# Chunked attention before a token mixer: batch 0's third tile reordered, and its first weights decoded later

## The chip, the cores and the metric

The kernel runs on one core of a Trainium2 chip. The metric is the device time of one execution in microseconds; it is compared between the kernel before and the kernel after. The engines are named as the profile names them: PE (matrix multiplications, with PEld for the loading of its weights), DVE (vector), ACT (activation), POOL and SP (which issues most of the DMA).

## The reference

Four batches of 8 heads, 768 positions, head size 64. Attention works in chunks of 32 positions, and what it gives goes through a token mixer of low rank and a two-layer network.

```
for each chunk of 32 positions c:
    k_full = [mem_k, k[c-16 : c+40]];  v_full = [mem_v, v[c-16 : c+40]]
    a = softmax(q_c @ k_full.T / 8)
    x[c] = a @ v_full
u   = x + (x.T @ U @ V).T          # U: 768x32, V: 32x768
out = u + relu(u @ w_ch1) @ w_ch2  # 512 -> 2048 -> 512
```

U, V, w_ch1 and w_ch2 reach the chip as 64-bit floats and are decoded on the chip, from two 32-bit words each, into a value that is held as a high part and a low part.

## The kernel before

The work is laid out in four batches. Batch 0's attention has the chip to itself at the start. From then on the network of a batch (`w1_step` and `w2_step`, lines 1235 to 1296) runs on PE while the attention of the next batch is woven into it. Products that need more than the low precision are done in three passes (high with high, high with low, low with high), so x's transposed form `u` and the weights both exist as a pair (`uh`, `ul`; `w1h`, `w1l`).

A batch has 6 blocks of 128 positions, taken in three tiles T = 0, 1, 2 of two blocks each. For a tile, `s_turn` makes the scores (line 551, 128 small matmuls on tiles of the PE array), `s_weights` the exponentials (L573 to L577), `s_sums` the row sums and their reciprocals (L582 to L587), `t_part` turns the exponentials in two calls (L605 on PE, L608 on ACT), and `av_part` makes the products with v (L624, again small matmuls, as many as for the scores) and scales them into two blocks of x on DVE (L635, four instructions). `collect(t)` adds block t of x times U into one bank (L647). V is decoded by `v_words` on ACT and DVE (L199, L206, L214, L219, L226) and spread over three groups of rows by `spread_v` (L251 on PE, L256 on ACT, L257 on DVE).

When all six blocks are collected, lines 921 and 922 split the sums into `g3`. The first half of u for the network (blocks 0 to 2) is then made in two steps: `turn_x` has turned x into four banks (L967), and `join_uT` adds V times g3 to them (L976) and splits each bank into `uh` (L980, ACT) and `ul` (L981, DVE). The second half (blocks 3 to 5) goes the same way by `turn_x1` (L991) and `join_uT1` (L1008, L1012, L1013); three of its four banks are done in the attention, the fourth in `joins`, inside the first `w1_step`.

The order of instructions on PE, ACT, DVE, POOL and SP is written out by hand here: an engine executes them in the order in which the program emits them. A waiting instruction holds back everything that comes after it on its engine. Three devices in this order matter:

- `keep_clock(n)` asks for n matmuls on zeros ahead of the next bank that is taken (L130). `GAP` and `CHAIN` hold the numbers.
- `bank()` gives out PSUM banks; while `wide[0]` is a number it goes round `cyc`, a list of seven entries over three pools, and with `None` it takes the three banks of `ps_a` alone.
- `stream()` decodes the network's weights, and `advance(n)` takes n steps of it. A word (one matrix of one f, or later both) goes through `begin` (ACT, L199), `shift` (DVE, L206), `power` (L214), `mantissa` (L219), `join` (L226), `upper` (ACT, L337: the high part) and `lower` (DVE, L341: the low part). Steps end where the code says `yield`. In the kernel before, `advance(5)` takes the first word through `join` and `upper` and begins the second; the two steps of `advance(2)` shift the second and make the first one's low part. `both_blocks` starts the network when `done[0]` says that both words of f = 0 are through.

The front's last part in the kernel before, in the order in which PE has it: scores of tile 2, `t_part(0)`, `av_part(0)`, `t_part(1)`, six matmuls on zeros, `av_part(1)`, `t_part(2)`, `collect` 0 to 3, `spread_v`, `turn_x`, two matmuls on zeros, `av_part(2)`, `collect` 4 and 5, two matmuls on zeros, `turn_x1` three times, then the joins.

Of the kernel before, what the change touches and what calls it, by code (L numbers as in the profile page):

```python
# [24 lines left out]
HEAD = {ET.Activation, ET.Pool}  # L25
FIRST = 3000
START = 12
GAP = [2, 2, 6, 2]
LOADS = 'mv t1 t2 uv v0 v1 v2 w0 w1 w2'
CHAIN = [2, 4]  # L30
WLO = 4
# [22 lines left out]
def chunk_attn_then_mixer_kernel(  # L54
# [56 lines left out]
    wide = [0]  # L111
# [15 lines left out]
    def att_ps():  # L127
        ps = bank()
        for _ in range(warm[0]):
            nc.tensor.matmul(out=ps, lhsT=busy[:, 0:P], rhs=busy, start=True, stop=True)  # L130
        warm[0] = 0
        return ps

    def keep_clock(n):

        warm[0] += n
# [110 lines left out]
    def spread_v(val):  # L247
        for g in range(VG):
            ps = att_ps()
            rows = slice(32 * g, 32 * g + 32)  # L250
            nc.tensor.matmul(  # L251
                out=ps[0:96, 0:VQ], lhsT=rep[rows].rearrange("p a b -> p (a b)"),
                rhs=val[rows, 0:VQ], start=True, stop=True,
            )
            c = slice(VQ * g, VQ * g + VQ)
            nc.scalar.copy(out=v3[:, c], in_=ps[0:96, 0:VQ])  # L256
            nc.vector.tensor_tensor(  # L257
                out=v3[32:64, c], in0=ps[32:64, 0:VQ], in1=v3[32:64, c].bitcast(F32), op=ALU.subtract,
            )
# [80 lines left out]
    def lower(f, which, val, hi, lo):  # L340
        nc.vector.tensor_tensor(out=lo, in0=val, in1=hi.bitcast(F32), op=ALU.subtract)  # L341
        if which == 0:
            unsaved.append((f, w1ls[f]))
        done[0] = 2 * f + which + 1

    done = [0]

    def stream():

        work = [[(f, n)] for f in range(NSOLO) for n in range(2)] + [[(f, 0), (f, 1)] for f in range(NSOLO, NF)]  # L350

        def ready(n):
            return n < len(work) and work[n][0][0] in staged and not (front[0] and len(work[n]) > 1)

        def begun(n):
            words = Words([raw for f, which in work[n] for raw in staged[f][which]], nc.vector, turn=n)
            words.begin()
            return words

        while not ready(0):  # L360
            yield
        ahead, before = begun(0), []
        yield
        for n, parts in enumerate(work):
            while ahead is None and not ready(n):
                yield
            if n + 1 == len(work):
                for part in before:
                    lower(*part)
                before = []  # L370
                yield
            words, ahead = ahead or begun(n), None
            words.shift()
            if before:
                yield
                for part in before:
                    lower(*part)
            if len(parts) > 1 and n + 2 < len(work) and ready(n + 1):
                ahead = begun(n + 1)
            yield  # L380
            words.power()
            yield
            words.mantissa()
            yield
            if ahead is None and n + 2 < len(work) and ready(n + 1):
                ahead = begun(n + 1)
            val = words.join()
            before = [(f, which, val[:, 512 * m:512 * m + 512]) for m, (f, which) in enumerate(parts)]
            before = [part + upper(*part) for part in before]
            yield  # L390
        for part in before:
            lower(*part)
        yield
# [3 lines left out]
    def advance(n):  # L397
        for _ in range(n):
            next(weights, None)
# [7 lines left out]
    def attention(b, xs):  # L407
# [129 lines left out]
        def s_turn(T):  # L537
            *_, last = s_halves(T)
            return last
# [39 lines left out]
        def s_sums(T):  # L579
            rs = rss[T] = sm.tile([P, 2, 2, 2, 2], F32, name="rs", bufs=3)  # L580
            for s in range(2):
                nc.vector.tensor_reduce(  # L582
                    out=rs[:, :, :, :, s].rearrange("n t g k -> n t k g"),
                    in_=pts[T, s].rearrange("n (t k g w) -> n t k g w", t=2, k=2, g=2), axis=AX.X, op=ALU.add,
                )
            nc.vector.tensor_scalar_add(out=rs, in0=rs, scalar1=1e-9)
            nc.vector.reciprocal(out=rs, in_=rs)  # L587
# [22 lines left out]
        def av_part(T):  # L610
            for _ in av_halves(T):
                pass
# [32 lines left out]
        def collect(t):  # L645
            if b == 0:
                nc.tensor.matmul(  # L647
                    out=gp[0][0:96], lhsT=u3[:, t].rearrange("p g r -> p (g r)"), rhs=xs[(b, t)],
                    start=(t == 0), stop=(t + 1 == NT),
                )  # L650
                return
            j = t % 4
            nc.tensor.matmul(  # L653
                out=gp[0][R * j:R * j + R, :], lhsT=u_sb[:, t, :], rhs=xs[(b, t)],
                start=(t < 4), stop=(t + 4 >= NT),
            )

        if b == 0:
# [59 lines left out]
            yield  # L718
            keep_clock(GAP[0])
            sc = s_turn(0)  # L720
# [7 lines left out]
            yield  # L728
            keep_clock(GAP[1])
            sc = s_turn(1)  # L730
# [14 lines left out]
            s_weights(2, *sc)  # L745
            v_words.begin()
            s_sums(1)
            av_part(0)
            yield
            for s in two:  # L750
                t_part(1, s)
            s_sums(2)
            keep_clock(GAP[2])
            av_part(1)
            for s in two:
                t_part(2, s)
            for t in two:
                collect(t)
            v_words.shift()
            v_words.low()  # L760
            val = v_words.join()
            yield
            for t in two:
                collect(2 + t)
            spread_v(val)
            early = turn_x(range(NCK))
            wide[0] = None
            keep_clock(GAP[3])
            av_part(2)
            yield  # L770
            advance(5)
            for t in range(4, NT):
                collect(t)
            keep_clock(CHAIN[0])
            turned.extend(turn_x1(c) for c in range(3))
            advance(2)
            yield
        else:
            mv = sm.tile([P, 4 * D], F32, name="mv")
# [139 lines left out]
        for c in range(0, CH, width):  # L919
# [3 lines left out]
                out=g3[64:96, cs], in0=gr[64:96, cs], in1=g3[64:96, cs].bitcast(F32), op=ALU.subtract,  # L923
            )
        if b == 0:
            join_uT(early, g3)
            for c in range(3):
                join_uT1(turned[c], c, g3)
            rest.extend((c, g3) for c in range(3, NCK))
            ranks.append(g3)  # L930
        yield "joined"
# [28 lines left out]
    def turn_x(cs):  # L960

        banks = []
        for c in cs:
            ps = ps_h.tile([P, 512], F32, name="ps_h") if c < 2 else ps_o.tile([P, 512], F32, name=f"acc{c - 2}")
            banks.append(ps)
            for tt in range(TB):
                nc.tensor.matmul(  # L967
                    out=ps[:, tt * P:(tt + 1) * P], lhsT=xs[(0, tt)][:, c * P:(c + 1) * P],
                    rhs=ident, start=(tt == 0), stop=False, skip_group_check=True,
                )  # L970
        return banks

    def join_uT(banks, g3):
        uht, ult = u_pair(0, 0)
        for c in range(NCK):
            nc.tensor.matmul(  # L976
                out=banks[c][:, 0:TOK], lhsT=g3[:, c * P:(c + 1) * P], rhs=v3[:, 0:TOK],
                start=False, stop=True, skip_group_check=True,
            )
            nc.scalar.copy(out=uht[:, c, :], in_=banks[c][:, 0:TOK])  # L980
            nc.vector.tensor_tensor(  # L981
                out=ult[:, c, :], in0=banks[c][:, 0:TOK], in1=uht[:, c, :].bitcast(F32), op=ALU.subtract,
            )

    turned, rest, ranks = [], [], []

    def turn_x1(c):

        ps = att_ps()
        for tt in range(TB):  # L990
            nc.tensor.matmul(  # L991
                out=ps[:, tt * P:(tt + 1) * P], lhsT=xs[(0, TB + tt)][:, c * P:(c + 1) * P],
                rhs=ident, start=(tt == 0), stop=False, skip_group_check=True,
            )
        return ps
# [8 lines left out]
    def join_uT1(ps, c, g3):  # L1004
        if (0, 1) not in uT:
            u_pair(0, 1)
        uh, ul = (a[c] for a in uT[(0, 1)])
        nc.tensor.matmul(  # L1008
            out=ps[:, 0:TOK], lhsT=g3[:, c * P:(c + 1) * P], rhs=v3[:, TOK:2 * TOK],
            start=False, stop=True, skip_group_check=True,  # L1010
        )
        nc.scalar.copy(out=uh, in_=ps[:, 0:TOK])  # L1012
        nc.vector.tensor_tensor(out=ul, in0=ps[:, 0:TOK], in1=uh.bitcast(F32), op=ALU.subtract)  # L1013
# [379 lines left out]
    head = ExitStack()  # L1393
    head.enter_context(tc.manual_schedule(engines=HEAD))
    first = attention(0, xs)
    base = tc.tile_snap_priority() - FIRST
    while True:
# [79 lines left out]
```

## Time and profile before

| what | value |
|---|---|
| median of 3 runs | 668.75 us (668.54, 668.75, 1119.33) |
| the profiled execution | 667.39 us |
| its span | 665.5 us |
| mean granted clock of PE | 0.991 |
| instructions profiled | 15136 |

The profiled execution is not one of the three runs. Its span lies between the first and the last profiled instruction; 1.9 us lie around it. Times in the trace are microseconds from the start of the span. A row of the timeline gives start, duration, engine, line, operation, output and inputs and how many were merged; in brackets stands how long the engine had been idle before and who ended that. The chain of waits follows the end of the program back through what released each step; "issue" there is time in which an engine waited for nothing that the profile shows. A row of the stretches gives, for each engine, busy time and count of instructions, and then PE's granted clock, the share of the DMA engines' time and what they moved.

### The profile page before, as it was taken

How to read it: one execution, taken by the hardware profiler on the slowest of the kernel's cores; microseconds unless marked ns; L12 is line 12 of the kernel's file. 1: busy time of each engine (PE TensorE's matmuls, PEld its weight loads, DVE VectorE, ACT ScalarE, POOL GpSimd, SP SyncE). 2: the span in 40 equal slices, each digit the busy share in tenths (PEclk: the TensorE clock that was granted, in tenths of full speed). 3: DMA queues.
4: the chain of work that ended last, by engine and by line, in shares of the span. 5: the costliest groups of instructions: out<-in, count | busy, mean ns of one | idle time of the engine just before them, and what ended most of it. 6: DMA issues, size and time to landing. Idle time of an engine off the chain costs nothing.

```text
span 665.5 us, 15136 instructions
## 1 busy us (share of the span) xinstructions
PE 641.1 (96%) x6192; PEld 559.4 (84%) x6192; DVE 343.1 (52%) x672; ACT 234.8 (35%) x574; POOL 72.6 (11%) x98
## 2 busy tenths in 40 slices
PE   8788999999979999999999989999999999999997
PEld 5557999998867898988878888999978899999886
DVE  6848788898552553435524733444536732222322
ACT  5526344447422244242322615332324512121221
POOL 5100000043000333051432000000000000000000
PEclk9899999999988999999999999999999999999999
DMA  8895366453850598456744378675523055555301
GB/s 235 154 330 197 126 203 204 129 160 113 161 133 18 173 290 249 109 171 218 235 159 158 128 230 248 188 198 138 158 79 111 1 158 167 157 157 160 120 1 47
DMA packets 121116, 105.98 MB, mean 159 GB/s; under 512 B 51192, under 2 KB 90616, under 8 KB 121048
## 3 DMA queue, kind: packets, MB, share of 16 engines
q1 hardware_dynamic: 120424, 104.87, 53.6%
q8 instruction: 49, 0.80, 0.5%
q10 hardware_dynamic: 624, 0.15, 0.1%
q14 instruction: 19, 0.16, 0.1%
HBM read 79.30 MB, written 25.17 MB: 157 GB/s over the span
## 4 chain that ended last, share of the span: by engine, by line
PE 88%; DVE 5%; DMA 2%; issue 2%; ACT 2%; SPq 0%; ACTq 0%; DVEq 0%
PE acc L1286 23%; PE ps_h L1235 19%; PE ps_h L1163 17%; PE acc L1296 11%; PE ps_a L624 2%; PE ps_a L492 2%; PE ps_a L551 2%; PE ps_a L1286 2%; PE ps_a L605 1%; DMA w1l<-w1s 1%; PE acc L1280 1%; PE ps_a L1296 1%; PE ps_a L653 1%; PE ps_a L1092 1%; PE ps_a L938 1%
## 5 line engine op out<-in xcount | busy, mean ns | idle before, releaser
L1286 PE MATMUL acc<-w,hh 128*128 128x512 f32 x606 | 158.6, 397 | 0.0
L1286 PEld LDWEIGHTS acc<-w,hh 128*128 128x128 f32 x606 | 110.6, 188 | 21.5 <-issue 1.3
L1296 PE MATMUL acc<-w,hl 128*128 128x512 f32 x303 | 87.4, 397 | 0.0
L1235 PE MATMUL ps_h<-uh,w1h 128*128 128x384 f32 x252 | 85.7, 342 | 0.6 <-ACT uh L1012 0.6
L1235 PE MATMUL ps_h<-ul,w1h 128*128 128x384 f32 x252 | 84.4, 337 | 0.4 <-DVE ul L1013 0.4
L1244 DVE SCALAR_TENSOR_TENSOR hl<-ps_h,hh 128x384 fp32r<-128x384 f32 x63 | 34.9, 555 | 78.2 <-ACT hh L1243 78.2
L1243 ACT ACTIVATE hh<-ps_h 128x384 fp32r<-128x384 f32 x63 | 30.9, 491 | 120.2 <-PE ps_h L1235 120.2
L1296 PEld LDWEIGHTS acc<-w,hl 128*128 128x128 f32 x303 | 55.6, 188 | 11.8 <-issue 0.8
L1235 PE MATMUL ps_h<-uh,w1l 128*128 128x384 f32 x252 | 55.0, 340 | 0.0
L1235 PEld LDWEIGHTS ps_h<-uh,w1h 128*128 128x128 f32 x252 | 47.2, 188 | 3.7 <-ACT uh L1012 0.9
L1235 PEld LDWEIGHTS ps_h<-ul,w1h 128*128 128x128 f32 x252 | 47.3, 188 | 3.2 <-DVE ul L1013 0.6
L1235 PEld LDWEIGHTS ps_h<-uh,w1l 128*128 128x128 f32 x252 | 45.1, 188 | 0.0
L1163 PE MATMUL ps_h<-t34h,w1l 128*128 128x384 f32 x128 | 39.4, 349 | 0.0
L1163 PE MATMUL ps_h<-t12h,w1l 128*128 128x384 f32 x128 | 37.2, 345 | 0.4 <-DMA w1l<-w1s 0.4
L1163 PE MATMUL ps_h<-bh,w1l 128*128 128x384 f32 x128 | 35.9, 340 | 1.5 <-DMA w1l<-w1s 1.5
L1180 DVE TENSOR_TENSOR c<-ps_h,c 128x384 f32<-128x384 f32 x16 | 8.9, 558 | 51.9 <-PE ps_h L1163 51.2
L1173 DVE SCALAR_TENSOR_TENSOR hl<-hst,hh 128x384 fp32r<-128x384 f32 x32 | 17.8, 556 | 27.8 <-PE acc L1296 27.7
L1049 POOL TENSOR_TENSOR vb<-w1h,w1l 128x512 f32<-128x512 f32 x16 | 20.8, 1302 | 90.8 <-DMA w1l<-w1ld 69.6
L1180 DVE TENSOR_TENSOR hst<-ps_h,hst 128x384 f32<-128x384 f32 x32 | 17.8, 555 | 24.1 <-ACT hst L1184 24.1
L1172 ACT ACTIVATE hh<-hst 128x384 fp32r<-128x384 f32 x32 | 16.8, 525 | 36.8 <-PE acc L1286 32.3
L1184 ACT COPY c<-ps_h 128x384 f32<-128x384 f32 x16 | 7.7, 480 | 51.9 <-PE ps_h L1163 51.9
L635 DVE TENSOR_TENSOR x<-ps_a,rs 128x256 f32<-128x256 f32 x42 | 15.0, 417 | 21.0 <-PE ps_a L624 21.0
(233 smaller groups left out, 1112.2 us busy)
## 6 DMA issues: line engine op xcount, KB each, us to landing
w1l<-w1s SPq DMA_DIRECT2D x112, 256.0 KB
w1l<-w1ld SPq DMA_DIRECT2D x35, 256.0 KB
w1s<-sums SPq DMA_DIRECT2D x32, 256.0 KB
rw<-in_moe_w_ch_dram SPq DMA_DIRECT2D x14, 512.0 KB
qraw<-in_q_dram SPq DMA_DIRECT2D x24, 256.0 KB
out_dram<-x SPq DMA_DIRECT2D x24, 256.0 KB
vb<-in_v_dram SPq DMA_DIRECT2D x56, 98.0 KB
raw<-in_moe_w_ch_dram SPq DMA_DIRECT2D x20, 256.0 KB
```

What stands on the lines that cost most here:

```text
L492: nc.tensor.transpose(out=psv[:, p, r, :], in_=half[:, r, 2 * p:2 * p + 2, :].rearrange("n h d -> n (h d)"), identity=ident,)
L635: nc.vector.tensor_tensor(out=x[:, 4 * D * g:4 * D * g + 4 * D].rearrange("n (j d) -> n j d", d=D), in0=psv[g][:, t], in1=rs[:, t, g].rear ...
L1049: nc.gpsimd.tensor_tensor(out=v2 if odd else v1, in0=hi, in1=lo, op=ALU.add)
L1163: nc.tensor.matmul(out=ps[:, :TOK], lhsT=w_, rhs=u, start=(start and m == 0), stop=(m == 5), skip_group_check=True,)
L1172: nc.scalar.activation(out=hh, in_=c, func=AF.Relu)
L1173: nc.vector.scalar_tensor_tensor(out=hl, in0=c, scalar=0.0, in1=hh.bitcast(F32), op0=ALU.max, op1=ALU.subtract,)
L1180: nc.vector.tensor_tensor(out=out, in0=ps[:, :TOK], in1=in1, op=ALU.add)
L1235: nc.tensor.matmul(out=ph[:, :TOK], lhsT=w[:, c, :], rhs=u[c], start=(m == 0), stop=(m + 1 == len(parts)),)
L1243: nc.scalar.activation(out=hh, in_=ph[:, :TOK], func=AF.Relu)
L1244: nc.vector.scalar_tensor_tensor(out=hl, in0=ph[:, :TOK], scalar=0.0, in1=hh.bitcast(F32), op0=ALU.max, op1=ALU.subtract,)
L1286: nc.tensor.matmul(out=acc[tt], lhsT=h[:, sl], rhs=w, start=(begins and m == 0), stop=False,)
L1296: nc.tensor.matmul(out=acc[tt], lhsT=hl[:, sl], rhs=w2h[f], start=False, stop=ends is not None)
```

## The change

In batch 0's attention PE gets a new order. `t_part(2)` and `collect` 0 and 1 come ahead of `av_part(1)`; `av_part(2)` comes ahead of `turn_x`. Five matmuls on zeros stand ahead of `av_part(0)` and two ahead of `t_part(2)`; the six ahead of `av_part(1)` and the two ahead of `av_part(2)` are gone. `av_part(2)` takes its banks from `cyc`, one entry further on, and `wide[0]` becomes `None` after it and not before.

The weight stream gets a new order too. Its first step (`begin` of the first word, on ACT) comes ahead of `av_part(2)`; `shift`, `power` and `mantissa` come after the last `collect`; `join` and `upper` come after the split of g3, ahead of `join_uT`; `lower` comes inside `join_uT`, after its second bank. The second word is not begun before `held[0]` is cleared, which is after the joins of the attention; so its `begin` and its `shift`, too, come after those. A new branch at the head of the stream's loop lets `lower` be a step of its own when no next word has been begun.

```diff
-GAP = [2, 2, 6, 2]
+GAP = [2, 2, 5, 2]
...
-    done = [0]
+    done, held = [0], [True]
...
         for n, parts in enumerate(work):
+            if ahead is None and before:
+                for part in before:
+                    lower(*part)
+                before = []
+                yield
             while ahead is None and not ready(n):
                 yield
...
-            if ahead is None and n + 2 < len(work) and ready(n + 1):
+            if ahead is None and n + 2 < len(work) and ready(n + 1) and not held[0]:
                 ahead = begun(n + 1)
...
             s_sums(1)
+            keep_clock(GAP[2])
             av_part(0)
             yield
             for s in two:
                 t_part(1, s)
             s_sums(2)
-            keep_clock(GAP[2])
-            av_part(1)
+            keep_clock(GAP[3])
             for s in two:
                 t_part(2, s)
             for t in two:
                 collect(t)
+            av_part(1)
             v_words.shift()
             v_words.low()
             val = v_words.join()
...
             for t in two:
                 collect(2 + t)
             spread_v(val)
+            advance(1)
+            wide[0] += 1
+            av_part(2)
+            wide[0] = None
+            yield
             early = turn_x(range(NCK))
-            wide[0] = None
-            keep_clock(GAP[3])
-            av_part(2)
-            yield
-            advance(5)
             for t in range(4, NT):
                 collect(t)
+            advance(3)
             keep_clock(CHAIN[0])
             turned.extend(turn_x1(c) for c in range(3))
-            advance(2)
             yield
...
         if b == 0:
+            advance(1)
             join_uT(early, g3)
             for c in range(3):
                 join_uT1(turned[c], c, g3)
+            held[0] = False
...
             nc.vector.tensor_tensor(
                 out=ult[:, c, :], in0=banks[c][:, 0:TOK], in1=uht[:, c, :].bitcast(F32), op=ALU.subtract,
             )
+            if c == 1:
+                advance(1)
```

## The prediction

> **What bounds the kernel now.** I first read the page's engine totals and DMA queues, then stretches of time, to see where PE stops being the limit (a row: stretch, length, busy us and instructions of PE, PEld, DVE, ACT and POOL, granted clock, DMA share, GB/s).
>
> ```profile
> PE 641.1 (96%) x6192; PEld 559.4 (84%) x6192; DVE 343.1 (52%) x672; ACT 234.8 (35%) x574; POOL 72.6 (11%) x98
> ...
> q8 instruction: 49, 0.80, 0.5%
> ```
>
> ```profile
> 56.00:60.00 4.00, 3.02 (x15) 2.36 (x14) 3.56 (x9) 1.94 (x4) 0.00 (x0) 1.00 0.02 7
> 60.00:150.00 90.00, 90.00 (x455) 81.89 (x454) 77.80 (x127) 40.95 (x88) 7.54 (x9) 1.00 0.51 164
> ```
>
> PE is busy 96% of the span. It has gaps up to 60 us and none from there to 150. All edits lie before. So the change is worth what it moves the moment from which PE has no more gaps; everything later shifts by the same. For that moment I read the chain of waits.
>
> ```profile
> 29.00 1.24 issue
> ...
> 31.85 2.58 issue
> ...
> 34.67 0.59 PE ps_a L605 x4
> 35.26 0.44 PE ps_h L605 x4
> 35.70 3.43 PE acc L647 x8
> ...
> 39.74 1.53 PE ps_h L967 x12
> 41.28 1.34 PE acc L967 x12
> ...
> 43.05 1.58 PE ps_a L624 x108
> 44.62 1.40 DVE x L635 x4
> ...
> 49.08 0.69 DVE w1l L341
> ...
> 49.80 0.43 DVE g L922
> ...
> 50.28 0.46 PE ps_h L976
> ...
> 51.34 1.95 DVE ul L981 x4
> ...
> 57.21 0.41 DVE w L341
> ...
> 57.82 0.56 DVE ul L1013
> ...
> 58.43 1.13 PE ps_h L1235 x5
> ```
>
> Three things hold PE up: 1.24 and 2.58 us with no releaser around `av_part(1)`; then the path from the last x (L635) over the weight stream to the split of g (L922); then, from the first join (L976) on, DVE's row of `ul`, word and last `ul`, at whose end (58.43) PE goes on for good.
>
> **The holes without a releaser are instruction fetches.** The stretch from one restart to the next, and the one after it:
>
> ```profile
> 34.40:41.55 7.15, 7.12 (x39) 4.31 (x40) 3.50 (x10) 2.86 (x8) 0.00 (x0) 1.00 0.93 298
> ...
> 30.20:34.40 4.20, 1.62 (x127) 1.46 (x127) 1.58 (x5) 0.00 (x0) 0.00 (x0) 1.00 0.60 130
> ```
>
> ```profile
> 34.43 0.24 PE L624 MATMUL acc<-vb,pt 64*32 64x64 f32 x1 [2.58 <-issue]
> ```
>
> Between the restarts at 30.24 and 34.43 PE ran 127 matmuls and 127 weight loads: 256 with two waits of its sequencer. Queue q8 carried 49 packets for the 12384 instructions of PE and PEld, 253 each. Now rows of the DMA view for three stretches: 31.6 to 33.1, 34.4 to 41.5, and 41.5 to 42.6.
>
> ```profile
> q8 instruction: 1, 0.02, 5.9%
> ```
>
> ```profile
> q1 hardware_dynamic: 1435, 2.11, 92.5%
> ```
>
> ```profile
> q8 instruction: 1, 0.02, 5.4%
> ```
>
> A packet came in the first stretch (5.9% of 16 engines over 1.5 us: 1.41 us long, so from 31.67 at the latest to 33.1); PE went on 1.34 us after its end. None came from 34.4 to 41.5, while q1 moved 2.11 MB; the next ran 0.95 us (5.4% over 1.1 us), from about 41.6. PE therefore works through a block of 256 while the next is on its way, and `av_part`, with its 256 in 1.6 us, outruns it. That limit stays; only what PE does between the blocks changes.
>
> **The change part by part.** Rows for its steps on PE, then on DVE:
>
> ```profile
> 24.82 0.30 PE L624 MATMUL ps_h<-vb,pt 64*32 64x64 f32 x2 [0.91 <-ACT pt L608]
> ...
> 27.54 1.46 PE L130 MATMUL ps_h<-busy 128*128 128x512 bf16 x6
> ...
> 45.41 1.96 PE L647 MATMUL acc<-x,uarea 128*96 128x512 f32 x4 [0.83 <-DVE x L635]
> ...
> 47.21 0.59 PE L130 MATMUL ps_a<-busy 128*128 128x512 bf16 x2
> 47.64 2.17 PE L991 MATMUL ps_a<-ident,x 128*128 128x128 f32 x18
> ```
>
> ```profile
> 35.72 0.28 DVE L206 TENSOR_SCALAR dec<-dec 96x256 int32<-96x256 int32 x1
> ...
> 36.81 0.42 DVE L226 TENSOR_TENSOR dec<-dec 96x256 f32<-96x256 f32 x1
> ```
>
> 1. *Five matmuls on zeros ahead of `av_part(0)`, two instead of six after `t_part(1)`.* Two start 0.215 us apart (0.43 from 47.21 to 47.64), so five take 1.08 us against an idle 0.91: cost 0 to 0.17. PE waits for the block at 30.24 in any case, so I take 0.
>
> 2. *`t_part(2)` and `collect` 0, 1 ahead of `av_part(1)`.* From 30.24: 0.59 + 0.44 for the turning, half of 3.43 for two collects; `av_part(1)` begins at 33.0. It needs the next block after some 230 of its 256 instructions, at 34.4, just when that comes (34.43). It ends at about 34.75, as before, with 2.75 us of work done inside the old hole. Then four L635 at 0.35 us and V's word 1.51 us (35.72 to 36.81 + 0.42): value at 37.65; `collect` 2 and 3 run beside it to about 37.3; spreading takes 0.61 (from L647's end at 39.13 to 39.74). `av_part(2)` starts at 38.3, not 43.05. These steps issue no DMA.
>
> 3. *`av_part(2)` meets the end of the next block.* After 28 left of `av_part(1)`, 8 of collects and 12 of spreading, some 204 of its 256 instructions are there: dry at 39.5. Let F be the start of the fetch: PE goes on at F + 0.95 + 1.34 and is through 0.45 later, at F + 2.74, and never before 38.3 + 1.58 = 39.9. Bounds for F: 35.9, if it comes 1.43 us after the restart like the one at 31.67 after 30.24 (then nothing stalls); 41.6, if the weight loads hold it as before. In the old order PE had done only some 80 instructions of its block when that fetch came (39 and 40 in 34.4 to 41.55, slow collects); the one at 31.67 came after 254. It looks as if the request follows progress into the block, not time. In the new order progress is held by V's value until 37.65; with 1.55 us on the way, near the 1.43, I take F = 39.2. `av_part(2)` ends at 41.95 instead of 44.63: 2.7 earlier.
>
> 4. *From there to the first join.* `turn_x` 2.8 (39.74 to 42.62, less an overlap), two collects 1.8 (45.41 to 47.21), two matmuls on zeros 0.43 and three `turn_x1` 2.1 now stand all in PE's row: 7.1 us. They hide L635, the stream's three steps and the split of g (two copies and two subtractions in turn, about 4 x 0.43 us after the collects, so 0.8 ahead of the join). L976 comes at 49.05 instead of 50.28: 1.23 earlier.
>
> 5. *DVE from the join on.*
>
> ```profile
> 54.60 0.42 DVE L214 TENSOR_SCALAR dec<-dec 128x512 int32<-128x512 int32 x1
> 55.05 0.69 DVE L219 SCALAR_TENSOR_TENSOR dec<-rw,dec 128x512 f32<-128x512 uint32 x1
> ```
>
> `lower` (0.60, as from L341 at 57.21 to 57.82) now stands between the second and third `ul`, and the second word's `shift` (0.45, as from L214 to L219, the same shape) ahead of that word's other steps. Both lay ahead of the join; now both lie on the chain to 58.43: +1.05. DVE is in order, so behind them wait two `ul`, three L1013, the second word and with it the last `ul`, for which PE waits. `join` and `upper` fall into the 0.8 us between g and L976, which about covers them; without it they would add up to 1.2. The second word's `begin` on ACT ends before DVE asks: 0.
>
> 6. *SP.* `lower` also releases the save of the first low weights on SP's queue:
>
> ```profile
> SPq L319 <- DVE w1l L341: 1.8, 1, 1.8
> ```
>
> That save comes about 1.7 us later, and one set of loads waits behind it. DMA is all but idle from 56 to 60 (share 0.02), so I cost it at nothing; without that slack, at 1.7.
>
> **Sum.** -1.23 + 1.05 = -0.2 us; in general the gain is 39.4 - F. Against the profiled execution (667.39 = span 665.5 + 1.9 around it) that makes 667.2. The runs' median, 668.75, stands 1.36 above that execution; what I predict for the runs is 668.55.
>
> **A rule against the change.** First rows from later in the chain, and the stretches behind them:
>
> ```profile
> 185.93 2.50 issue
> ...
> 196.92 2.04 issue
> ```
>
> ```profile
> 189.80:193.10 3.30, 3.30 (x10) 2.61 (x11) 3.14 (x7) 1.20 (x2) 0.40 (x1) 0.50 0.90 317
> ...
> 200.10:203.30 3.20, 3.20 (x12) 2.71 (x11) 1.23 (x4) 1.08 (x2) 0.00 (x0) 0.50 0.34 82
> ```
>
> Each of these holes in PE was followed by a stretch at half clock; the one of 2.58 at 31.85 was not. [...]
>
> **The rivals.**
>
> *A, the fetch is not late.* With F at 37.1 or earlier `av_part(2)` ends at 39.9 and the gain is 39.4 - 37.1 = 2.3: 666.4. For it: the fetch at 31.67. Against: the one at 41.6. [...]
>
> *B, slower: the fetch stays where it was.* The weight loads, not progress, set F = 41.6. The work moved ahead then only lengthens a later wait: `av_part(2)` ends at 44.3, `turn_x` and the collects still follow, L976 comes at 51.4 and DVE pays its 1.05: +2.2, 670.95. It decides from F = 39.4 on, and the change then doesn't do what it says. For it: 2.11 MB of q1 at 92.5% in the stretch without a fetch. Against: only some 80 instructions done in it.
>
> *C, slower: half clock.* [...] For it: 2.04. Against: 2.58 without it.
>
> **How the numbers follow.** Forecast 0.4 (F from 38 to 40.5: 667.35 to 669.85), A 0.3, B 0.15, C 0.15. For 8 in 10 the range takes in A and B and a little for the scatter between profile and median: 666.0 to 671.2; C on top of B is left out. Two per cent, about what a measurement of this kernel can tell from no change, is 13.4 us, more than any case here: faster by that 0.01, slower 0.01, within 0.98.
>
> **What would show it.** Right: no hole at 31.85, `t_part(2)` at 30.3, `av_part(2)` at 38.3 with a hole near 39.5, a q8 packet near 39.2, L976 near 49, PE without gaps from about 58.2. F at 36 or at 41.6 shows A or B; half clock between 40 and 47 shows C. The step from L976 to the end of the last `ul` (8.1 before, 9.15 expected) tests the DVE term. A new hole after 60, or loads that PE waits for, would make the sum wrong altogether.

## The result, and the profile after

The changed kernel is slower: 671.81 us in the median of 18 runs (668.94 the lowest) beside 668.64 of the kernel before (18 runs), a ratio of 1.0055 with a 95% interval of 1.0032 to 1.0077. That is within the 2% that the chances speak of, but the time lies 0.6 us above the range 666.0 to 671.2, and the sign is wrong: forecast was a gain of 0.2 us. The profiled execution took 670.4 us (span 668.5, mean granted clock 0.991), 3.0 more than that of before. Medians are of all runs; the ratios leave out runs in a slow state (here one of 1119.33 us before and one of 1951.24 us after) and are not the quotients of the medians. Other runs of the kernel before, made beside each group of experiments, had medians from 666.7 to 668.8; so experiments are compared by ratios.

Lines have moved by 5 to 10: L551, L605, L624, L635, L647, L967, L976, L981, L1013 and L1235 of before are now L556, L610, L629, L640, L652, L975, L984, L989, L1023 and L1245; in the experiments' kernels they lie up to 13 lines further on or back. From the chain of waits of the changed kernel (start, length, what):

```profile
40.24 4.46 issue
...
45.37 2.86 PE ps_h L975 x12
48.22 1.91 PE acc L975 x12
50.14 1.73 PE acc L652 x4
...
53.60 0.70 DVE dec L226
...
54.38 0.62 ACT w1h L337
55.00 0.38 ACT uh L988
...
55.48 1.02 DVE ul L989 x2
56.50 0.60 DVE w1l L341
57.10 0.66 DVE ul L989 x2
...
63.02 0.56 DVE ul L1023
...
63.62 0.96 PE ps_h L1245 x4
```

The hole at 31.85 is gone. In its place stands one of 4.46 us in `av_part(2)`, and everything behind it has moved: PE goes on for good at 63.62 instead of 58.43. Now four stretches (length, busy us and count of PE, PEld, DVE, ACT and POOL, granted clock, DMA share, GB/s), and rows of the DMA view for 35.0 to 42.2 and for 42.2 to 43.3:

```profile
30.55:35.00 4.45, 4.25 (x127) 2.71 (x127) 1.01 (x3) 1.07 (x2) 0.00 (x0) 1.00 0.77 178
35.00:42.20 7.20, 4.13 (x127) 2.08 (x126) 3.83 (x11) 1.57 (x5) 0.00 (x0) 1.00 1.02 358
...
42.50:49.20 6.70, 4.50 (x44) 4.33 (x45) 2.94 (x8) 0.00 (x0) 0.00 (x0) 0.50 1.05 390
...
64.00:150.00 86.00, 86.00 (x435) 78.30 (x434) 73.81 (x123) 39.25 (x85) 4.13 (x4) 1.00 0.51 164
```

```profile
q1 hardware_dynamic: 1665, 2.58, 102.0%
```

```profile
q8 instruction: 1, 0.02, 5.2%
```

From the restart at 35.00 PE ran its whole block (253 of the 256 are in the trace) without a packet coming. The packet began at 42.25, 7.25 us behind the restart; before it had been 41.60 and 7.17 us. So the fetch kept its distance to the restart, although PE's work in between had changed altogether. Then the clock was halved from 42.5 to 49.3, just where `turn_x` now stands. From 64 on PE has no gaps, as before.

A second profile of the same kernel shows that this isn't one bad execution.

> The changed kernel once more, for a second profile of it. If its late packet is a thing of the kernel and not of one execution: the packet that fills the end of av_part(2) between 41.5 and 43.5 us, 6.5 to 8 us behind the restart of the block before it, hole 3.5 to 5.5 us, first low part of U (L989) between 54.5 and 56.5. If it was one bad execution: packet below 39, hole below 1 us.

Measured: packet at 41.51 (7.18 us behind the restart at 34.33), hole 4.19 us, half clock from 42.4 to 49.2, first low part of U at 54.92. So the late packet belongs to the kernel.

### The profile page after: what moved, and what is told of

It reads as the page before. It is cut to its first block, busy times and chain, and to the rows that moved or that the text cites. A ratio compares the mean times of both kernels' runs of the same rounds, so it can differ in the third digit from the quotient of the medians.

```text
span 668.5 us, 15144 instructions
## 1 busy us (share of the span) xinstructions
PE 640.2 (96%) x6191; PEld 558.8 (84%) x6191; DVE 343.1 (51%) x672; ACT 234.5 (35%) x574; POOL 73.6 (11%) x98
## 4 chain that ended last, share of the span: by engine, by line
PE 83%; DVE 6%; DMA 3%; SPq 2%; issue 2%; ACT 2%; ACTq 0%; POOL 0%; DVEq 0%; POOLq 0%
PE acc L1296 22%; PE ps_h L1173 18%; PE ps_h L1245 17%; PE acc L1306 11%; PE ps_a L497 2%; PE ps_a L629 2%; PE ps_a L556 2%; SPq L479 1%; PE ps_a L610 1%; PE ps_a L1296 1%; DVE vb L219 1%; PE acc L1290 1%; PE ps_a L658 1%; DVE vb L226 1%; DMA w1l<-w1s 1%
## 5 line engine op out<-in xcount | busy, mean ns | idle before, releaser
L1245 PE MATMUL ps_h<-uh,w1h 128*128 128x384 f32 x252 | 85.8, 342 | 1.0 <-ACT uh L1022 1.0
L1245 PE MATMUL ps_h<-ul,w1h 128*128 128x384 f32 x252 | 84.4, 337 | 0.4 <-DVE ul L1023 0.4
L1245 PE MATMUL ps_h<-uh,w1l 128*128 128x384 f32 x252 | 55.1, 341 | 0.0
L1245 PEld LDWEIGHTS ps_h<-uh,w1h 128*128 128x128 f32 x252 | 47.2, 188 | 4.2 <-ACT uh L1022 1.4
L1245 PEld LDWEIGHTS ps_h<-ul,w1h 128*128 128x128 f32 x252 | 47.3, 188 | 3.2 <-DVE ul L1023 0.6
L1245 PEld LDWEIGHTS ps_h<-uh,w1l 128*128 128x128 f32 x252 | 45.1, 188 | 0.1
L1173 PEld LDWEIGHTS ps_h<-bh,w1l 128*128 128x128 f32 x128 | 23.5, 188 | 3.2 <-issue 2.6
```

What stands on the lines that cost most here:

```text
L1173: nc.tensor.matmul(out=ps[:, :TOK], lhsT=w_, rhs=u, start=(start and m == 0), stop=(m == 5), skip_group_check=True,)
L1245: nc.tensor.matmul(out=ph[:, :TOK], lhsT=w[:, c, :], rhs=u[c], start=(m == 0), stop=(m + 1 == len(parts)),)
```

## The experiments

In the following, "restart" is the moment at which PE comes to the first instruction of the block of 256 that holds the end of `av_part(1)`; "ready" is how long that block had been landed by then, and "packet" the start of the next fetch. A restart is called starved when PE had run dry and goes on as soon as it can (at this block 1.26 to 1.60 us behind the landing). The numbers are from the trace's lists of PE's instructions and of q8's packets.

**The two halves of the change.** First PE's order alone: the changed kernel with this edit, and without `held` and the new branch of the stream. Then the order of the decoding alone: the kernel before with the same lines the other way round, `held` and the branch.

```diff
             spread_v(val)
-            advance(1)
             wide[0] += 1
...
+            advance(5)
             for t in range(4, NT):
                 collect(t)
-            advance(3)
             keep_clock(CHAIN[0])
             turned.extend(turn_x1(c) for c in range(3))
+            advance(2)
...
-            advance(1)
             join_uT(early, g3)
...
-            if c == 1:
-                advance(1)
```

> The changed order of PE with the weight stream in its old order (advance(5) after av_part(2), advance(2) behind turn_x1, no held). If the hole in av_part(2) and the half clock behind it are the main cause: the hole stays (fetch near 42, 4.5 us), the step from the first join to the last ul falls from 9.6 to about 8.2, 1.4 us faster than the changed kernel: near 670.3, still 1.5 or more slower than before. If the later weights are the main cause: back to 668.6 or below.

> The old order of PE with the weight stream in its new order (begin early, three steps after the collects, join and upper behind the split of g, lower inside the join, the second word held back). No hole in av_part(2), fetch near 41.6. The split of g comes 1.3 us earlier, but PE's row of turn_x1 lets the join come only 0.5 us earlier (49.8); the step from the join to the last ul grows from 8.15 to 9.3 to 9.6. Sum +0.7 to +1.0 us: 669.3 to 669.7. If the later weights are the main cause of the changed kernel's loss: 671 or more. If DVE's steps are hidden after all: 668.1.

Measured: PE's order alone 670.74 us, ratio 1.0021 (0.9992 to 1.0051); packet at 43.97, 7.17 us behind its restart at 36.79, half clock from 37.4 to 44.2. The hole is split there, since the packet before was late too: 2.88 us ahead of 36.79 and 2.07 in `av_part(2)`. From the first `ul` to the end of the last it takes 7.03 us (56.39 to 63.42). The decoding's order alone 666.50 us, ratio 0.9955 (0.9927 to 0.9983): faster than the kernel before, where a loss had been expected. From its chain (L988 and L1022 are L989 and L1023 of the changed kernel):

```profile
51.44 1.02 DVE ul L988 x2
52.46 0.60 DVE w1l L341
53.06 0.67 DVE ul L988 x2
...
58.98 0.56 DVE ul L1022
```

From the first `ul` to the end of the last it takes 8.10 us (51.44 to 59.54) and before 7.04 (51.34 to 58.38). So the loss on DVE is there, 1.06 us, as in the changed kernel (55.48 to 63.58: 8.10), and absent with PE's order alone. The gain must lie elsewhere.

**Where the decoding's order wins.** SP's queue before and after 160 us, first of the kernel before:

```profile
156.98 7.90 SPq L319 DMA_DIRECT2D w1ld<-w1l  x2
...
165.69 1.59 SPq L456 DMA_DIRECT2D vb<-mv  x2
167.33 2.48 SPq L474 DMA_DIRECT2D vb<-in_v_dram  x4
```

Batch 1's loads of v stand behind the saves of the last two units' low parts of W1, 7.90 us, most of it for the second, which isn't decoded yet. In the changed kernel (163.20) and in the one with the decoding's order alone (159.05) these loads come first. So the kernel before got only this (the argument names a unit whose save is kept for the next call):

```diff
     def fetch_w1l(f):
-        save_w1l()
+        save_w1l(NF - 1 if f == NF - 5 else None)
```

> The kernel before with one edit: the save of the last unit's low part of W1 (the fetch for unit 11 doesn't send it) goes to SP's queue behind batch 1's first loads of v, where the changed kernel and the one with the order of the decoding alone have it. In the kernel before SP stands 7.90 us on that save from 156.98 with the loads of v behind it. Theory S (this is where the order of the decoding alone won its time, 0.9955): loads of v from 157 instead of 165.7, PE's stretch from block 11 to block 19 of its instructions 57.5 to 59.5 us instead of 61.58, median 2 to 3.4 us below the kernel before, ratio 0.995 to 0.997. Theory of chance (holes and half-clock windows between 180 and 206 fall differently in each kernel): ratio 0.999 to 1.001 and a stretch anywhere between 57 and 62.

```profile
157.13 0.34 SPq L323 DMA_DIRECT2D w1ld<-w1l  x1
...
158.05 1.60 SPq L461 DMA_DIRECT2D vb<-mv  x2
159.69 3.29 SPq L479 DMA_DIRECT2D vb<-in_v_dram  x4
...
165.84 0.35 SPq L323 DMA_DIRECT2D w1ld<-w1l  x1
```

Measured: 666.89 us, ratio 0.9974 (0.9948 to 1.0001); the loads come 7.6 us earlier and PE's stretch from block 11 to block 19 takes 58.37 us instead of 61.58. Its chain has one hole there, instead of the 2.50 and 2.04 us of before:

```profile
193.88 1.88 issue
```

Over all kernels whose blocks lie alike, that stretch takes 57.33 to 59.85 us with the late save (eight profiles) and 59.66 to 61.58 without it (three): 1.6 us in the mean. These kernels differ in more than the save, and the stretches at half clock fall differently in each (two between 189 and 204 us in the kernel before, one in the changed kernel). The time points the same way, but its interval just touches no change. So theory S is borne out in direction, at about 1.7 us; why the decoding's order alone gained 3.0 in spite of its 1.06 isn't covered by that, and stays open within the intervals.

**Does the packet only stand behind the weights?** In both kernels the first three weight units were held back on SP until x of block 2 is there, so that the queues should be empty at the restart.

```diff
+            def hold(t):
+                held_d = dram.tile([1, 16], F32, name="held")
+                nc.sync.dma_start(out=held_d, in_=xs[(b, t)][0:1, 0:16])
...
-            take(len(loading))
+            take(1)
...
             av_part(1)
+            hold(2)
+            take(len(loading))
```

> The changed kernel, with the loads of the first three weight sets held back on SP behind a tiny DMA that reads x of block 2, so that they begin only after av_part(1). Theory Q (the fetch of the next block of PE's instructions is queued behind the weight transfers that were issued before it): without them it starts 1.5 to 2.5 us after PE's restart near 35, at 36.5 to 37.5; av_part(2) has no hole and ends near 40.7 instead of 45.4, no half clock follows, the first join comes near 48 and the last ul near 57.5 instead of 63.6: 664.5 to 666.5 us, faster than before by 2 to 4. Theory P (the request follows PE's progress into the block, which V's value holds up): the fetch starts at 40.2 or later, a hole of at least 2.5 us stays in av_part(2), and the time is 668 to 671 us.

> The kernel before with the same holding back of the weight loads. PE's order is untouched, so in the block that begins at 34.4 it still does only some 80 instructions in the next 7 us. Q: the fetch nevertheless starts at 36 to 37 instead of 41.6. P: it starts at 40 to 41.6 as before. The time should hardly move by either (within 1 us of before, 668.6), since av_part(2) reaches the end of its block only at 43.8; if the weights come late instead, up to 2 us slower.

Measured: the changed kernel with it 670.62 us, ratio 1.0024 (0.9999 to 1.0050), packet at 43.07; the kernel before with it 668.31, ratio 0.9991 (0.9968 to 1.0014), packet at 41.07. The DMA view of the first for 34.5 to 36.4, and where PE goes on:

```profile
q1 hardware_dynamic: 2, 0.00, 0.1%
```

```profile
45.54 0.31 PE L629 MATMUL ps_a<-vbe,pt 64*32 64x64 f32 x1 [5.83 <-issue]
```

The restart was at 34.46. For 1.9 us nothing but two small packets was on the way, and no fetch came; it came 8.61 us behind the restart, with a hole of 5.83 us, as theory P had it. That speaks against queueing alone. It doesn't exclude it: after other starved restarts the packet comes up to 2.0 us behind, and here the weights were on their way by then. The block at 191.99 us, below, decides it. The kernel before doesn't test the question: there x of block 2 is ready ahead of the restart at 34.34, and the weights run again from 33.6 on (DMA share 0.85 to 34.34, and 1.01 in the 2 us behind).

**Does the request follow PE's progress?** That was the forecast's reason. Here 48 small instructions are put where PE waits for x, so that it passes the point in question before V's value is there; in a second kernel the weights are held behind V's value; a third has both. `nudge(n)` adds n products of 32x4 zeros onto the sums of `collect`, which changes nothing in them; `hold` is a 64-byte transfer that reads `v3`.

```diff
             av_part(1)
+            nudge(24)
...
             spread_v(val)
+            hold()
+            take(len(loading))
```

> The changed kernel with 24 products of 32 by 4 zeros, 48 instructions of PE, added behind the second group's products with v, onto the sums that the collects build, where PE waits for x anyhow. Theory P (the packet of the next 256 instructions is asked for only when PE's queue has passed some fifty or sixty instructions of the running block, and in the changed kernel it stands before that point on the waits for x and for V's value): the point is passed near 35.3 us instead of 39.0, the packet comes between 36.4 and 38.5 instead of 42.25, and the hole of 4.46 us in av_part(2) falls to between 0 and 1.2 us; no half clock at 42.5; the first low part of U (L989) starts near 51.5 instead of 55.48, and the median is 2 to 5 us below the changed kernel's 671.8. Theory Q (the packet is asked for at the restart and stands behind the weights): packet at 42 as before, hole 4.5 us or more, median as the changed kernel's. All later blocks begin 48 instructions earlier, so that the holes of batch 1 move too: the verdict is read from the front.

> The changed kernel with the loads of the first three weight units held on SP behind a 64-byte transfer that reads V's spread value, so that no weight stands in the queues when PE passes the point of theory P. Theory P with queueing behind it: asked for near 39.0, the packet comes 1.1 to 1.6 us later, at 40.1 to 40.6, hole 2.3 to 2.8 us instead of 4.46. P without queueing (the time from asking to landing is long for another reason): packet at 42 again, hole near 4.5. The weights start near 41 instead of 32; if the first units come late for their decoding, the first low part of W1 moves behind 58 and part of the gain is lost: median between 667 and 671.

> Both: the 24 zero products and the weights held behind V's value. P with queueing: asked for near 35.3 with idle queues, packet at 36.4 to 36.8, no hole over 0.3 us in av_part(2). If queueing alone counts: as the held kernel, 40 to 42. If the packet keeps to about 7 us after the restart whatever is done: 42.

Measured: with the small instructions 667.92 us, ratio 1.0020 (0.9991 to 1.0049); packet 4.54 us behind its restart (41.18 after 36.64), no hole in `av_part(2)`, but 2.61 us ahead of it, since the packet before was late as well, with half clock from 36.0 to 42.8 and the first `ul` at 52.52. That is earlier, and still later than theory P's figure. With the weights held behind V's value 665.96 us, ratio 0.9966 (0.9942 to 0.9990): faster than before, no hole, first `ul` at 50.72. With both 668.18, ratio 0.9999 (0.9977 to 1.0021), no hole there either. In the held kernel the packet came 0.99 us behind the restart at 35.80. Its DMA view for 35.80 to 37.75, and PE's row:

```profile
q8 instruction: 1, 0.02, 2.9%
```

```profile
37.03 0.67 PE L652 MATMUL acc<-x,uarea 128*96 128x512 f32 x1 [0.86 <-DVE x L640]
```

The packet began at 36.78, before PE had got past the first 29 instructions of its block, which end in the wait for x. So progress by fifty or sixty instructions is not needed in this case, and theory P falls as it was put. But the empty queue need not be all of it: for 1.9 us it was empty in the changed kernel held behind x as well. What differed: here PE came to the block 2.91 us after it had landed, there 1.38 us after, that is as soon as PE goes on at all.

> The changed kernel with the first weights held behind V's value once more. In its first profile the packet came 0.99 us behind the restart, but there the half clock at 30.9 had also made PE slow ahead of it, so that the block had landed 2.91 us before PE came to it. Theory H (the empty queues do it): packet within 1.5 us of the restart again, even where the block before is needed within 1.6 us of its landing. Theory N (it is asked for at once only where PE wasn't starved at the restart): where PE was starved, packet 2 to 6 us behind the restart, yet without the 2 to 4 us that weights add.

The second profile (667.13 us) again had no starved restart (ready 3.00, packet 0.95 behind), so it couldn't separate the two theories. In all four profiles with the weights held behind V's value (the one with both edits and one further down among them) PE ran at half clock for 3.4 us between 30.1 and 35.7, ahead of this restart; none of them shows a starved restart with empty queues.

**Starved or not.** The last pair leaves the weights where they are. One kernel gets 1.7 us of added zero products ahead of `av_part(1)`, so that PE comes late to the block; the other, the control, has `nudge(8)` at that place: the same 16 instructions in 0.28 us.

```diff
                 collect(t)
+            keep_clock(8)
             av_part(1)
```

> The changed kernel with eight zero products of 512 columns ahead of av_part(1), some 1.7 us of PE, so that the next block has landed 2.5 us or more before PE comes to it, while the weights stand in the queues as in the changed kernel. Theory N: packet 1 to 3.5 us behind the restart (near 37.5 to 40), hole below 1 us. Theory H: 6 us or more behind the restart, packet at 42.5 or later, hole 3 us or more.

> The control for the slowed kernel: 8 products of 32 by 4 zeros, the same 16 instructions at the same place, but only some 0.2 us of PE. The boundaries of the instruction blocks lie where they lie in the slowed kernel, yet PE comes to the next block within 1.7 us of its landing. Theory N: packet 6 us or more behind the restart, near 41.5 to 43, hole 3 to 5 us. If the place of the boundary had done it: packet within 4 us of the restart, hole below 1 us.

> The changed kernel with the eight zero products of 512 columns ahead of av_part(1), as profiled once before (first low part of U at 51.33 us instead of 55.48, hole in av_part(2) 0.68 us instead of 4.46), now timed. Theory N (a restart at which PE was starved gets the next packet late): about 4 us of the front are won back for 1.7 us of added zero work, so the median lies 2.5 to 4.5 us below the changed kernel's 671.8, at 667.3 to 669.3, ratio to the kernel before 0.998 to 1.001. If the one profile was a lucky execution: median 670 to 672, ratio 1.002 to 1.006, and a packet near 42 in this profile.

The chain of the slowed kernel, then of the control (L975 and L989 of the changed kernel are L976 and L990 in the one, L982 and L996 in the other; L691 is `nudge`):

```profile
33.96 1.73 PE ps_a L130 x8
...
41.91 0.68 issue
...
43.12 1.53 PE ps_h L976 x12
44.65 1.34 PE acc L976 x12
45.99 1.73 PE acc L652 x4
...
51.33 1.02 DVE ul L990 x2
```

```profile
33.02 0.28 PE acc L691 x8
...
40.02 4.50 issue
...
45.36 2.86 PE ps_h L982 x12
48.21 2.02 PE acc L982 x12
...
55.58 1.02 DVE ul L996 x2
```

With 1.7 us more work on PE the first `ul` comes 4.2 us earlier (one run of each: 668.62 and 671.80 us). The stretch from 42.8 to 49.5 in the same two kernels:

```profile
42.80:49.50 6.70, 6.65 (x77) 5.34 (x59) 3.82 (x11) 0.74 (x2) 0.00 (x0) 1.00 1.06 396
```

```profile
42.80:49.50 6.70, 4.99 (x54) 4.82 (x54) 2.94 (x8) 0.00 (x0) 0.00 (x0) 0.50 1.02 386
```

The slowed kernel, with a hole of 0.68 us, keeps the whole clock there (1.00); the control, with one of 4.50 us, has half of it (0.50). Timed, the slowed kernel has 664.88 us, ratio 0.9968 (0.9945 to 0.9991), faster than the kernel before; its second profile (the slowest of its 12 runs, 669.1) had its packet at 41.99, but 4.21 us behind a restart that came at 37.78; the hole in `av_part(2)` was 1.24 us, and the clock stayed whole behind it (`turn_x` 2.87 us there too, 44.82 to 47.69). Over all profiles:

| kernel | ready, us | packet behind the restart, us |
|---|---|---|
| before, and held behind x | 1.34, 1.26 | 7.17, 6.74 |
| before with the decoding's order, with the late save | 1.44, 1.26 | 6.54, 7.08 |
| changed, twice, and control | 1.55, 1.60, 1.43 | 7.25, 7.18, 7.46 |
| only PE's order | 1.57 | 7.17 |
| changed, held behind x | 1.38 | 8.61 |
| changed, 48 small instructions | 1.26 | 4.54 |
| changed, slowed, twice | 2.84, 3.77 | 3.60, 4.21 |
| changed, held behind V's value, twice | 2.91, 3.00 | 0.99, 0.95 |
| the same with 48 small instructions | 3.20 | 1.00 |
| the parts together (below), held; slowed | 3.35; 3.27 | 0.78; 3.50 |

At this block there are two terms. When PE enters it starved (ready up to 1.60), its successor comes 4.5 to 8.6 us later; when it has lain 2.8 us or more, in 0.8 to 4.2. And of the latter the weights in the queues make up 2.6 to 3.3 us (3.60 and 4.21 beside 0.95 and 0.99).

What asks for the packet stays open. Starving alone isn't the condition: the blocks that PE entered at 20.95, 25.21 and 30.23 in the kernel before had been ready for 1.90, 1.68 and 1.46 us and had the next packet 1.4 to 2.0 us later. The block behind the one in question was entered with ready 1.29 to 1.82 in twelve profiles, all with the weights still in the queues, and its successor came 2.5 to 3.8 us later. A wait of PE isn't the condition either: in the changed kernel PE stops some 30 instructions behind the restart to wait for x and V's value, but in the kernel before it was busy for 7.12 of the 7.15 us. And a queue isn't needed at all. In batch 1 of the kernel with the 48 small instructions PE entered a block at 191.99 (ready 1.60); the DMA view is for 191.99 to 197.7:

```profile
191.99 0.32 PE L556 MATMUL ps_a<-kall,qt 64*32 64x64 f32 x9 [1.76 <-issue]
```

```profile
DMA packets 0, 0.00 MB, mean 0 GB/s; under 512 B 0, under 2 KB 0, under 8 KB 0
```

PE worked on without a wait, nothing was on the way on any queue, and the packet began at 197.73, 5.74 us behind the restart, when PE had done 67 instructions. That would fit a request that follows progress. But in the changed kernel the block entered at 30.55 (ready 1.30) had its packet 1.97 us later, with 26 instructions done. None of the three, queue, wait and progress, explains all of these by itself.

**The parts together.** PE's order of the changed kernel, the decoding's order of the kernel before and the late save, once with the weights held behind V's value and once with the slowing zeros.

> PE's order of the changed kernel, the order of the decoding of the kernel before, the first weights held behind V's value, and the last save of W1's low part behind batch 1's first loads of v: each part that won time in a run, without the 1.06 us that the decoding between the low parts of U cost. If the parts add: first low part of U near 50.7, the last one ends near 57.8 instead of 58.37, the second batch's stretch 57.5 to 59.5 instead of 61.58: median 664 to 665.5, ratio 0.993 to 0.996. If the first unit's decoding, which this order puts ahead of the join, has to wait for the held weights: first low part of U at 52 or later and ratio 0.997 or more.

> PE's order of the changed kernel with the eight zero products ahead of av_part(1), the decoding in the order of the kernel before, and the last save of W1's low part behind batch 1's first loads of v; no weights held. If the parts add: first low part of U near 51.3, the last one ends 7.0 us later near 58.4 as in the kernel before, the gain is that of the save alone: median 665 to 667.5, ratio 0.994 to 0.998. If the decoding ahead of the join delays the split of g as in the kernel before: first low part of U 52 or later, ratio 0.998 to 1.001.

Measured: held 665.93 us, ratio 0.9974 (0.9953 to 0.9995), first `ul` at 50.93, the last one's end at 58.08: less than the sum, since PE waits 1.61 us (48.26) ahead of the join for a decoding that waits for held weights. Slowed 664.54 us, ratio 0.9951 (0.9927 to 0.9974), the best of all. From its chain:

```profile
40.80 0.68 issue
...
56.32 0.56 DVE ul L1021
```

Its last `ul` ends at 56.88, 1.5 us earlier than before (58.38). So in this profile PE's new order is worth that much in the front, its 1.7 us of zeros included, once the packet comes in time.

## Why the prediction was wrong

Its steps in turn:

- **Steps 1 and 2 were right but for 0.6 to 0.7 us.** No hole at 31.85, the turning of tile 2 from 30.76, V's value at 38.28 (forecast 37.65, the restart itself being 0.57 late), `av_part(2)` from 39.02 (38.3).
- **Step 3 failed: it had the fetch 3.05 us too early.** It took F = 39.2, that is V's value at 37.65, at which the request was to go out, and 1.55 us on the way. F was 42.25, 3.97 behind V's value. Shown are two terms that the step didn't have. With 1.7 us more work ahead of the restart the packet comes 3.60 us behind it, and in the control with the same 16 instructions 7.46: at this block it matters whether PE enters it starved. And of the 3.60 to 4.21 the weights in the queues are 2.6 to 3.3; the 1.55 left them out: the fetch at 31.67, beside which it was set, began ahead of the first weights (issued at 31.78). Whether the request itself follows progress, as the step had it, stays open. The observation behind it (254 and some 80 instructions done at the two fetches of the kernel before) was true but two points. `av_part(2)` also ended 0.38 later than F + 2.74 says (45.37 instead of 44.99).
- **Rival B had nearly the right F, for half the reason.** F = 41.6 (42.25 measured) was put down to the weights alone, which are 2.6 to 3.3 us of the delay. **Rival C came on top of it**, which the range left out: `turn_x` took 4.77 us (45.37 to 50.14) instead of the 2.87 in the slowed kernel (43.12 to 45.99), +1.90. The prediction has B and C as two cases (0.15 each), but they come together: each of the four holes over 4 us in `av_part(2)` (4.19, 4.46, 4.50 and 5.83) went with 6.8 us at half clock. How long a hole must be for that isn't shown: the 2.61 us of the kernel with 48 small instructions went with 6.8 us at half clock too, and the 2.58 us of the kernel before with none (clock 1.00 from 30.20 to 41.55).
- **Step 4** was 7.1 us from there to the first join; at full clock it is 6.79 (43.12 to 49.91), -0.31. The joins in the slowed and in the changed kernel:

```profile
49.91 0.59 PE L985 MATMUL ps_h<-v,g 96*128 96x384 f32 x2
```

```profile
54.05 0.59 PE L984 MATMUL ps_h<-v,g 96*128 96x384 f32 x2
```

- **Step 5 was right in its term and short beside it.** The first `ul` to the end of the last: 8.10 instead of 7.04, +1.06 for 1.05. But `join` and `upper` were not quite covered: L337 (54.38 to 55.00) stands ahead of L988 on ACT while PE has the join at 54.05, and first `ul` comes 1.43 behind the join instead of 1.06: +0.37.
- **Sum of the front:** -0.18 (the forecast, -1.23 + 1.05) + 3.05 + 0.38 + 1.90 - 0.31 + 0.37 = +5.21; measured 63.62 - 58.43 = +5.19.
- **Step 6 looked at the wrong save.** The first save at 56 cost nothing, as said. But the order shifts every save, and the last one now lets batch 1's loads of v pass: they start at 163.20 instead of 165.69, though PE had come to be 5.19 later. The changed kernel's holes there are shorter:

```profile
187.70 0.73 issue
...
192.20 0.78 issue
199.99 1.91 issue
```

By block 19 of PE's instructions (223.88 before, 226.79 after) the 5.19 have shrunk to 2.91; that and 0.07 behind it make the 2.98 us of span. "Everything later shifts by the same" was therefore wrong by 2.3 us, of which the late save is an estimated 1.6 to 1.7, from the comparisons above.

## What to carry to other kernels

Where PE works through many small instructions, find in the trace when each block of them lands and when PE enters it: behind a starved entry the next packet can be microseconds late (4.5 to 8.6 us behind the restart at the block here), and a little useless work ahead of the entry can be cheaper than the hole (here 1.73 us of zeros, and a hole of 0.68 us instead of 4.46). Price a hole like the one of 4.46 us here, ahead of a long run of matmuls, with the half clock that went with it (6.8 us of it, +1.90 us in `turn_x`). And when a reordered stream shares a queue with later loads that wait behind it, as batch 1's loads of v stood behind two saves for 7.90 us on SP's, look at the whole length of that queue for what it passes, not only at the edit.

## What the hardware showed beside that

- `av_part` took 204 instructions of a block in 1.01 us (39.02 to 40.03 in the changed kernel), while the next packet took 0.92 us and PE went on 1.53 us behind its end (1.26 to 1.60 at the starved restarts of the table). That packet began at 42.25, after PE had run dry at 40.24; the hole is 4.46 us.
- With empty transfer queues a fetch still came 5.74 us behind its restart (at 191.99, in the kernel with 48 small instructions); at the block in question the packet came 0.95 and 0.99 us behind the restart with the weights held, and 3.60 and 4.21 with the weights in the queues and PE slowed, 2.6 to 3.3 us more.
- 1.73 us of products on zeros took the changed kernel from a ratio of 1.0055 to the kernel before to 0.9968.
